# A planned attention-and-experts kernel: VectorE's two-operand steps, triangles by select, the 1e-9 and the sinks' products

## The chip, the cores and the metric

The kernel runs on one core of a Trainium2 chip. The metric is device time in microseconds of one execution. Before the change it is 349.83 us, the median of three runs (349.22 to 351.33).

A core has TensorE (PE, with PEld for its weight loads), VectorE (DVE), ScalarE (ACT), GpSimd (POOL) and SyncE (SP), which here only issues DMAs. Each engine works through its own instructions in program order and waits on semaphores for the others.

## What is computed

Two stages in float32. The first is attention with four sink keys and a window of 128 keys, for 4 batches and 8 heads of 64 over 768 positions. The second, over its output, is four causal attention experts of width 64, of which each row takes the two with the largest gate logits.

```python
keep = is_sink | in_window                      # 4 sinks, window 128
scores = np.where(keep, scale * q @ k.T, -1e9)
a = np.exp(scores - scores.max(-1))
a = a / (a.sum(-1) + 1e-09)
x = a @ v                                       # heads side by side: 768 x 512
...
topk = np.argpartition(-(x @ w_gate), 2)[..., :2]
w = np.exp(sel - sel.max(-1)); w /= w.sum(-1) + 1e-09
for e in range(4):                              # causal attention of each expert
    a = softmax_causal(scale * (x @ wq[e]) @ (x @ wk[e]).T)   # sum + 1e-09 too
    out += mask_e * w_e * (a @ (x @ wv[e]) @ wo[e])
```

## The kernel before

**Stages.** A unit of the first stage is a batch and a pair of heads (16 units): load q, k and v, turn them so that the head dimension lies on the partitions (on TensorE in batch 0, L679; by VectorE's 32x32 transposes later, L698), compute scores (L709 for rows 0 and 1, L726 for two rows at a time in the band), pick and mask on VectorE (L1113, L1119, L1057), exponentiate on ScalarE with the row sum (L1123, L1062), take the reciprocal (`factor`), normalise on GpSimd (L1143, L1077), turn the probabilities and multiply with v (L753). The result goes as a high and a residual part into x: L588 on ScalarE, L593 on VectorE. A unit of the second stage is a batch and a pair of experts: projections from x (L1232, three float32r products of high and residual parts each), scores (L717), mask (L975), exponential (L987), normalisation, products (L753), output projection (L1308) and store. Values and gate logits of all experts come from L1259.

**Weights.** Each weight is split as it arrives: ScalarE writes the high part (L531), then GpSimd or VectorE subtracts it from the staged weight to give the residual part (L538). In that subtraction both operands are in SBUF.

**The sum's reciprocal.** `factor` runs after every group of exponentials, 88 times. Its `go` on VectorE is a tensor_reduce (L772), which adds the row sum in column 1 of a small tile `st` to a constant 1e-9 in column 4, and then a reciprocal (L773). In the second stage a small GpSimd multiplication with the gate's weight follows (L776).

**The triangles.** Of a band's two key blocks, the nearer is needed once whole and once cut to its triangle. In 8 row pairs of batch 0 (`transposed_band`) TensorE turns the block and a select on GpSimd (L869, 128x256) or a multiplication on VectorE (L872) cuts it. The other 24 row pairs (`swapped_band`, batches 1 to 3) turn it by VectorE and a trip through DRAM; there one multiplication of 128x512 with a mask `swapped_own` cuts it (L921), 18 times on GpSimd and 6 times on VectorE.

**The sinks' products.** `of_sinks` (L758) adds the four sink keys' part: one or two matmuls of 128 lanes, of which lanes 64 and up hold zeros.

**The gate.** `weigh` (L1290 to L1294, VectorE) turns the kept logits' exponentials into weights; L1290 and L1294 have two SBUF operands. `rank` (L1281 and after, GpSimd) stands before it.

**What sets the order.** All work is cut into 2427 steps with a cost per engine that may run them. `ORDER` is a list of all steps' numbers; a letter behind a number puts the step on ScalarE (a), VectorE (v) or GpSimd (p) instead of the engine that its cost names first. `Plan.emit` goes through the list in order and writes each step's instructions into its engine's program; beside that it keeps a clock of its own from the costs, which decides only which buffer of a ring a step takes and where dummy matmuls fill TensorE's gaps in the first 130 us.

Of the kernel before, what the change touches and what calls it, by code (L numbers as in the profile page):

```python
# [10 lines left out]
F32 = mybir.dt.float32  # L11
# [3 lines left out]
OP = mybir.AluOpType  # L15
AX = mybir.AxisListType
# [146 lines left out]
class Step:  # L163


    def __init__(self, prio, cost, fn, after, new, use, moves, mode, behind, lag, besides, spared):
# [4 lines left out]
        for b in new:  # L171
            b.maker = self
# [15 lines left out]
class Plan:  # L188
# [1236 lines left out]
```

## Time and profile before

| | before |
|---|---|
| median of three runs | 349.83 us |
| the profiled execution | 349.71 us, span 348.0 us |
| TensorE busy | 337.1 us (97%) |
| VectorE busy | 294.4 us (85%) |
| ScalarE busy | 263.0 us (76%) |
| GpSimd busy | 210.8 us (61%) |
| TensorE's granted clock | 0.998 |
| DMA moved | 65.44 MB, 188 GB/s |

The span is the time from the first to the last instruction in the trace; 1.7 us of the execution lie around it. A row of the timeline gives start, duration, engine, line, operation, the tiles written and read, and in brackets how long the engine stood idle before it and who ended that. A row of a group gives total busy time, the mean of one in nanoseconds, and the idle time of the engine before its instructions. TensorE's matmuls are pipelined, so their durations overlap.

### The profile page before, as it was taken

The page shows a single profiled execution, that of the slowest core. Times are in us where ns is not written, and L with a number is a line of the kernel's source. Part 1 is how long each engine was busy: PE and PEld are TensorE (multiplying, and loading weights), DVE is VectorE, ACT ScalarE, POOL GpSimd, SP SyncE. Part 2 cuts the span into 40 slices and gives each one's busy share as a digit, 9 for nine tenths or more (in the row PEclk, how much of TensorE's full clock was granted, in tenths as well). Part 3 has the DMA queues.
Part 4 walks back from the last instruction along what each step waited for, and adds up shares of the span by engine and source line. Part 5 has one row for each costly group of instructions (what it writes and reads, how often), then busy time and mean ns, then how long its engine had stood idle before and what let it go on. Part 6 is the DMA issues. An engine that isn't in the chain of part 4 may idle for free.

```text
span 348.0 us, 12460 instructions
## 1 busy us (share of the span) xinstructions
PE 337.1 (97%) x4290; PEld 291.3 (84%) x4290; DVE 294.4 (85%) x1245; ACT 263.0 (76%) x874; POOL 210.8 (61%) x411
## 2 busy tenths in 40 slices
PE   8899899998989999999999999999999999999996
PEld 7677688986888799987888889977898899987885
DVE  5899999999899998899999888899987875579712
ACT  3899999968987986668969686499858964679922
POOL 7699798877767564677952734288984600144600
PEclk9999999999999999999999999999999999999999
DMA  7798799996977879769385989969785582037785
GB/s 232 176 218 130 104 153 170 202 208 182 235 221 187 238 190 198 210 147 166 114 267 136 190 244 167 218 174 229 250 252 158 197 259 65 2 122 216 224 277 194
DMA packets 159318, 65.44 MB, mean 188 GB/s; under 512 B 115856, under 2 KB 148880, under 8 KB 159256
## 3 DMA queue, kind: packets, MB, share of 16 engines
q1 hardware_dynamic: 158984, 64.53, 73.6%
q8 instruction: 34, 0.56, 0.7%
q14 instruction: 28, 0.23, 0.2%
q10 hardware_dynamic: 272, 0.13, 0.1%
HBM read 39.69 MB, written 24.90 MB: 186 GB/s over the span
## 4 chain that ended last, share of the span: by engine, by line
PE 78%; DVE 11%; ACT 3%; DMA 2%; issue 2%; POOL 1%; SPq 1%; DVEq 0%; ACTq 0%; POOLq 0%
PE b L1232 18%; PE b L753 17%; PE b L1259 10%; PE b L1308 9%; PE b L717 9%; PE b L784 5%; PE b L726 5%; PE b L709 2%; PE b L679 2%; DMA d<-n 2%; DVE p L1119 1%; PE b L758 1%; ACT n L1062 1%; DVE n L975 1%; DMA p<-d 1%
## 5 line engine op out<-in xcount | busy, mean ns | idle before, releaser
L1123 ACT ACTIVATE p<-p,st 128x132 f32<-128x132 f32 x128 | 50.9, 403 | 6.0 <-DVE st L1119 6.0
L1062 ACT ACTIVATE n<-n,st 128x128 f32<-128x128 f32 (+1 forms) x96 | 42.8, 449 | 4.9 <-DVE st L1057 4.9
L1077 POOL TENSOR_TENSOR n<-n,st 128x256 f32<-128x256 f32 (+2 forms) x50 | 35.0, 716 | 11.1 <-DVE st L773 9.1
L987 ACT ACTIVATE n<-n,st 128x768 f32<-128x768 f32 (+1 forms) x32 | 28.0, 876 | 16.4 <-DVE st L975 12.9
L717 PE MATMUL b<-ks,qs 64*128 64x384 f32 (+3 forms) x384 | 38.1, 333 | 0.9 <-DVE ks L653 0.9
L1259 PE MATMUL b<-wvh,x 128*128 128x260 f32 x192 | 36.6, 285 | 0.0
L753 PE MATMUL b<-n,v 128*64 128x128 f32 x544 | 34.7, 275 | 0.0
L1232 PE MATMUL b<-x,wqh 128*128 128x512 f32 (+1 forms) x128 | 33.5, 345 | 1.0 <-DVE st L975 1.0
L1308 PE MATMUL b<-woh,y 128*128 128x512 f32 (+1 forms) x100 | 34.2, 396 | 0.0
L1232 PE MATMUL b<-x,wkh 128*128 128x512 f32 (+1 forms) x128 | 33.7, 345 | 0.0
L1143 POOL TENSOR_TENSOR p<-p,st 128x512 f32<-128x512 f32 x32 | 33.2, 1040 | 0.0
L717 PEld LDWEIGHTS b<-ks,qs 64*128 64x128 f32 x384 | 30.2, 186 | 3.5 <-DVE ks L653 1.0
L605 ACT ACTIVATE n<-b 128x384 f32<-128x384 f32 (+2 forms) x65 | 27.5, 446 | 6.5 <-PE b L784 4.1
L1119 DVE CUSTOM_DVE_ANT_0 p<-b,pair_mask 128x132 f32<-128x132 f32 x128 | 32.1, 283 | 0.3
L753 PEld LDWEIGHTS b<-n,v 128*64 128x64 f32 x544 | 30.0, 137 | 2.3 <-issue 0.7
L824 DVE STREAM_TRANSPOSE n<-n 128x768 f32<-128x768 f32 (+1 forms) x32 | 28.3, 898 | 3.0 <-ACT n L995 3.0
L1259 PEld LDWEIGHTS b<-wvh,x 128*128 128x128 f32 x192 | 30.3, 188 | 0.7 <-DVE st L1057 0.4
L921 POOL TENSOR_TENSOR p<-p,swapped_own 128x512 f32<-128x512 f32 x18 | 23.3, 1295 | 11.4 <-DMA p<-d 10.4
L726 PE MATMUL b<-n,n 64*64 64x200 f32 (+1 forms) x512 | 27.0, 336 | 2.9 <-DVE x L593 1.5
L605 ACT ACTIVATE p<-b 128x256 f32<-128x256 f32 (+1 forms) x56 | 23.9, 449 | 7.7 <-PE b L1308 5.3
L698 DVE STREAM_TRANSPOSE n<-n 128x384 f32<-128x384 f32 x48 | 26.3, 560 | 2.4 <-DMA n<-in_k_dram 1.2
L1259 PE MATMUL b<-wvl,x 128*128 128x260 f32 x96 | 27.1, 282 | 0.0
(147 smaller groups left out, 1006.8 us busy)
## 6 DMA issues: line engine op xcount, KB each, us to landing
d<-n SPq DMA_DIRECT2D x24, 288.0 KB, 2.9
n<-in_v_dram SPq DMA_DIRECT2D x16, 384.0 KB, 4.6
p<-d SPq DMA_DIRECT2D x96, 64.0 KB, 2.5
d<-n SPq DMA_DIRECT2D x16, 384.0 KB, 2.6
n<-d SPq DMA_DIRECT2D x64, 96.0 KB, 2.8
out_dram<-p SPq DMA_DIRECT2D x23, 256.0 KB, 2.9
d<-n SPq DMA_DIRECT2D x16, 320.0 KB, 2.9
n<-d SPq DMA_DIRECT2D x64, 80.0 KB, 2.8
```

What stands on the lines that cost most here:

```text
L605: nc.scalar.activation(dst(), src(), AF.Copy)
L717: nc.tensor.matmul(o, self.qs.t[hs, a, qs], x, start=n == 0, stop=n == 2)
L726: nc.tensor.matmul(o[c:c + 64, 256 * r:256 * r + n], self.q_of()[hs, q:q + 64], self.ks.t[hs, 0, k:k + n], start=True, stop=True)
L753: nc.tensor.matmul(o[e * 64:e * 64 + 64], lhs, rhs, start=e not in self.begun, stop=last and self.done == len(self.steps))
L1062: nc.scalar.activation(x, x, AF.Exp, bias=st.t[:, 0, n:n + 1], scale=-1.0, accum_out=st.t[:, 1, n:n + 1])
L1077: nc.gpsimd.tensor_mul(x, x, f[:, :, None].to_broadcast([128, n, 128 * i + 128]))
L1119: nc.vector.tensor_tensor_reduce(out=p.t[:, n, :], in0=s2[e].t[:, 324 * r:324 * r + SW], in1=pair_mask, scale=-scale, scalar=BIG, op0=OP.a ...
L1123: nc.scalar.activation(p.t[:, n, :], p.t[:, n, :], AF.Exp, bias=st.t[:, 0, n:n + 1], scale=-1.0, accum_out=st.t[:, 1, n:n + 1])
L1143: nc.gpsimd.tensor_mul(p.t[:, :, :128], p.t[:, :, :128], f()[:, :, None].to_broadcast([128, 4, 128]))
L1232: nc.tensor.matmul(t.t, w[a][:, c, es], X[b, c].t[:, x, cs], start=c == 0 and m == 0, stop=c == NCH - 1 and m == 2)
L1259: nc.tensor.matmul(t.t[:, :VW], X[b, c].t[:, a, qs], W["wv"][w][:, c, :], start=c == 0 and n == 0, stop=c == NCH - 1 and n == 2)
L1308: nc.tensor.matmul(t.t[:, a0:z0], Y[b, c].t[:, a, qs], W["wo"][w][:, c, a0:z0], start=c == 0 and n == 0, stop=c == EP - 1 and n == 2)
```

## The change

Five things.

1. The planner's clock now treats a VectorE step with two SBUF operands (`port=True`: residual weights, the sinks' residual values, the gate's weights) as one that starts only when GpSimd's clock is free, and that keeps GpSimd for its length. The costs of these steps are smaller: 330 for 620, 1200 for 1900, 1000 for 1045.
2. The swapped rows' triangles are cut by two selects of 128x256 on GpSimd (L932 after the change); the mask `swapped_own`, its four copies and the option of VectorE go.
3. `factor` is two steps: a tensor_scalar that adds 1e-9 (L776 after the change), on VectorE or GpSimd, and the reciprocal on VectorE (L779). The list puts 39 of the 88 on VectorE and 49 on GpSimd.
4. A step of the sinks' products may carry the letter q: then it takes 64 lanes and counts as the tile shape of the score matmuls. 16 of the 32 carry it.
5. `ORDER` is a new list, of 2514 steps (88 more, and the mask's step less).

```diff
-46 4 48 54 55v 47 49 51 58 61 56v 132 52v 57 62v 53a 60a 66 59v 63a 67 134 71 133 218 69 140 137 304 73 139v 82 135 138v 83
+47 3 45 46 53 50 55a 48 51v 136 134 57 135 60 52a 54v 62a 58a 56 59v 61v 65 66 139 68 70 67 72 82 223 1 141a 83 88 69 142 108
...
-                s = self.steps[int(word.rstrip("avp"))]
+                s = self.steps[int(word.rstrip("avpq"))]
+                if word[-1] == "q":
+                    s.mode, s.cost = s.alt[0], {PE: s.alt[1]}
...
+            if e == DVE and s.port:
+                t = max(t, free[POOL])
+                free[POOL] = t + s.cost[e]
...
-    def mask_of_swapped():
-        for g in range(2):
-            for e in range(2):
-                to = swapped_own.rearrange("p (g h) (r e) c -> p g e h r c", g=2, r=2)[:, g, e]
-                nc.gpsimd.tensor_copy(to, own.rearrange("p (r h c) -> p h r c", r=2, h=2))
...
-                me.append(plan.step(prio + 3, {POOL: 160 + 2.05 * w + 190 * extra, DVE: 620 + 90 * extra}, low, after=[h], use=[st]))
+                me.append(plan.step(prio + 3, {POOL: 160 + 2.05 * w + 190 * extra, DVE: 330 + 90 * extra}, low, after=[h], use=[st], port=True))
...
-            nc.tensor.matmul(self.b.t[:, at:at + n], lhs, rhs, start=not self.begun, stop=last and self.done == len(self.steps))
+            nc.tensor.matmul(self.b.t[:, at:at + n], lhs[lanes], rhs[lanes], start=not self.begun, stop=last and self.done == len(self.steps))
...
+        def guard():
+            on = nc.gpsimd if guarded.eng == POOL else nc.vector
+            on.tensor_scalar(st.t[:, 2, :w], st.t[:, 1, :w], 1e-9, None, op0=OP.add)
+
         def go():
-            r = st.t[:, 2, :w]
-            nc.vector.tensor_reduce(r, st.t[:, 1:5:3, :w].rearrange("p r e -> p e r"), axis=AX.X, op=OP.add)
-            nc.vector.reciprocal(r, r)
-        s = plan.step(prio, {DVE: 285}, go, after, (), [st])
+            nc.vector.reciprocal(st.t[:, 2, :w], st.t[:, 2, :w])
+        guarded = plan.step(prio, {DVE: 140, POOL: 150}, guard, after, (), [st])
+        s = plan.step(prio, {DVE: 145}, go, [guarded], (), [st])
...
+            lanes = slice(0, 64 if wide.mode == "rows" else 128)
...
         def tri():
-            flat = lambda x: x.rearrange("p q n c -> p (q n c)")
-            (nc.gpsimd if cut_off.eng == POOL else nc.vector).tensor_mul(flat(pts[1].t), flat(pts[0].t), flat(swapped_own))
-        cut_off = plan.step(prio, {DVE: 70 + 1.04 * 512, POOL: 1250}, tri, [came] + OWN, [pts[1]], [pts[0]])
+            for g in range(2):
+                half = slice(2 * g, 2 * g + 2)
+                nc.gpsimd.affine_select(out=pts[1].t[:, half], in_=pts[0].t[:, half], pattern=[[32, 2], [64, 2], [0, 2], [1, 32]],
+                                        compare_op=OP.is_ge, fill=0.0, base=0, channel_multiplier=-1)
+        cut_off = plan.step(prio, {POOL: 800}, tri, [came], [pts[1]], [pts[0]])
...
-            WT_READY[b] += [[plan.step(prio, {DVE: 1045}, weigh, [s], (), [gate])]] * m
+            WT_READY[b] += [[plan.step(prio, {DVE: 1000}, weigh, [s], (), [gate], port=True)]] * m
...
-    SELECT_NS = 410
+    SELECT_NS = 375
```

Lines after L760 have moved by up to 12: L593 is L597, L698 is L702, L872 is L879, L1077 is L1089, L1113 is L1125 and L1119 is L1131 after the change.

VectorE before, where the residual of wk is made while batch 0's first stage runs (`x` is that stage's output, `st` the small tile of sums, `n` and `p` rows of scores or probabilities, `b` PSUM banks):

```order
L772 TENSOR_REDUCE st_126<-st_126 128x4
L773 RECIPROCAL st_126<-st_126 128x4
L698 STREAM_TRANSPOSE n_76<-n_76 128x384
L538 TENSOR_TENSOR wkl<-v_0_108,wkh 128x256
L593 SCALAR_TENSOR_TENSOR x_103<-b_128,x_103 128x512
L1119 ISA p_98,st_122<-b_131,pair_mask 128x132
L1119 ISA st_122 128x1
L698 STREAM_TRANSPOSE n_76<-n_76 128x384
L538 TENSOR_TENSOR wkl<-v_0_108,wkh 128x256
```

The same place after:

```order
L779 RECIPROCAL st_126<-st_126 128x4
L879 TENSOR_TENSOR p_85<-b_134,own 128x2x2x64
L879 TENSOR_TENSOR p_85<-b_129,own 128x2x2x64
L702 STREAM_TRANSPOSE n_79<-n_73 128x3x128
L1125 COPY_PREDICATED b_132<-nearer,b_132 128x2x64
L542 TENSOR_TENSOR wkl<-v_0_108,wkh 128x256 x2
L1125 COPY_PREDICATED b_135<-nearer,b_135 128x2x64
L597 SCALAR_TENSOR_TENSOR x_103<-b_128,x_103 128x256
L776 TENSOR_SCALAR st_127<-st_127 128x4
L779 RECIPROCAL st_127<-st_127 128x4
```

Three single subtractions, two of them next to a residual of x, became two in a row (the other two of wk are GpSimd's now), and the reduce before a reciprocal became a tensor_scalar, here or on GpSimd.

GpSimd before, where the first swapped triangles of batch 1 are cut and the gate of batch 0 is ranked:

```order
L1077 TENSOR_TENSOR n_69<-n_69,st_127 128x256
L1077 TENSOR_TENSOR n_75<-n_75,st_126 128x512
L1077 TENSOR_TENSOR n_69<-n_69,st_127 128x512
L921 TENSOR_TENSOR p_90<-p_95,swapped_own 128x512
L1023 TENSOR_TENSOR p_98<-n_68 128x512
L921 TENSOR_TENSOR p_82<-p_80,swapped_own 128x512
L1281 TENSOR_TENSOR gate_119<-gate_119 128x24
```

And after:

```order
L1089 TENSOR_TENSOR n_76<-n_76,st_123 128x256
L776 TENSOR_SCALAR st_126<-st_126 128x2
L1027 TENSOR_TENSOR vs_117<-vp,sel 64x128
L1089 TENSOR_TENSOR n_76<-n_76,st_123 128x512
L776 TENSOR_SCALAR st_124<-st_124 128x4
L776 TENSOR_SCALAR st_122<-st_122 128x2
L932 AFFINE_SELECT p_85<-p_80 128x256 x2
L1035 TENSOR_TENSOR p_90<-n_74 128x512
L1293 TENSOR_TENSOR gate_119<-gate_119 128x24
```

Each multiplication with the mask became two selects, and three small tensor_scalar stand between GpSimd's multiplications.

## Rows read from the trace of the kernel before

**Rows 1.** The page's first part: busy time, share of the span, instructions.

```profile
PE 337.1 (97%) x4290; PEld 291.3 (84%) x4290; DVE 294.4 (85%) x1245; ACT 263.0 (76%) x874; POOL 210.8 (61%) x411
```

**Rows 2.** Stretches: length, busy PE, PEld, DVE, ACT, POOL, clock, DMA share, GB/s.

```profile
0.00:12.00 12.00, 9.53 (x247) 8.21 (x251) 7.24 (x43) 5.72 (x20) 8.14 (x41) 1.00 0.84 231
...
24.00:36.00 12.00, 11.67 (x239) 9.18 (x237) 11.37 (x66) 12.00 (x54) 11.69 (x28) 1.00 0.96 146
36.00:48.00 12.00, 10.46 (x163) 8.11 (x158) 11.87 (x48) 10.36 (x46) 9.87 (x22) 1.00 0.80 128
...
180.00:192.00 12.00, 12.00 (x182) 10.92 (x179) 11.56 (x49) 9.49 (x28) 3.97 (x4) 1.00 0.64 172
...
336.00:348.00 12.00, 8.73 (x61) 6.87 (x59) 2.44 (x6) 2.45 (x5) 0.00 (x0) 0.95 0.60 221
```

**Rows 3.** TensorE's waits: for whom, us in total, times, longest.

```profile
PE b L726 <- issue: 1.3, 1, 1.3
PE b L1325 <- DVE nought L394: 1.1, 1, 1.1
```

**Rows 4.** Timeline of VectorE, 36 to 43 us.

```profile
36.74 2.93 DVE L538 TENSOR_TENSOR wkl<-v,wkh 128x256 fp32r<-128x256 f32 x1
39.59 0.68 DVE L593 SCALAR_TENSOR_TENSOR x<-b,x 128x512 fp32r<-128x512 f32 x1
...
40.90 0.38 DVE L538 TENSOR_TENSOR wkl<-v,wkh 128x256 fp32r<-128x256 f32 x1
```

**Rows 5.** Timeline of GpSimd, 18 to 40 us.

```profile
18.03 1.41 POOL L869 TENSOR_SCALAR_AFFINE_SELECT p<-p 128x256 f32<-128x256 f32 x1
...
36.34 1.11 POOL L869 TENSOR_SCALAR_AFFINE_SELECT p<-p 128x256 f32<-128x256 f32 x3
37.43 1.60 POOL L1077 TENSOR_TENSOR n<-n,st 128x256 f32<-128x256 f32 x2
38.99 0.40 POOL L869 TENSOR_SCALAR_AFFINE_SELECT p<-p 128x256 f32<-128x256 f32 x1
```

**Rows 6.** Timeline of TensorE: the three places where VectorE ends its wait.

```profile
40.33 0.54 PE L726 MATMUL b<-n,n 64*64 64x196 f32 x5 [1.54 <-DVE x L593]
...
80.85 0.74 PE L1232 MATMUL b<-x,wqh 128*128 128x512 f32 x2 [0.99 <-DVE st L975]
...
113.40 0.44 PE L753 MATMUL b<-p,p 128*64 128x128 f32 x4 [0.46 <-DVE p L921]
```

**Rows 7.** Timeline of VectorE and GpSimd around the gate's weights.

```profile
78.16 1.03 DVE L1290 SCALAR_TENSOR_TENSOR gate<-gate 128x24 f32<-128x24 f32 x1
...
78.11 1.04 POOL L1143 TENSOR_TENSOR p<-p,st 128x512 f32<-128x512 f32 x1
...
304.51 0.18 DVE L1290 SCALAR_TENSOR_TENSOR gate<-gate 128x24 f32<-128x24 f32 x1 [0.16 <-POOL gate L1286]
```

**Rows 8.** Groups by line and shape: busy us, mean ns, idle time before.

```profile
L758 PEld LDWEIGHTS b<-sk,vs 128*128 128x128 f32 x56 | 8.6, 189 | 3.1 <-issue 2.2 <-DVE st L975 0.2
...
L772 DVE TENSOR_REDUCE st<-st 128x4 f32<-128x8 f32 x56 | 8.4, 150 | 1.3 <-ACT p L1123 0.7 <-POOL p L1143 0.2
...
L869 POOL TENSOR_SCALAR_AFFINE_SELECT p<-p 128x256 f32<-128x256 f32 x14 | 6.4, 479 | 0.0
...
L921 DVE TENSOR_TENSOR p<-p,swapped_own 128x512 f32<-128x512 f32 x6 | 6.1, 1023 | 0.0
...
L776 POOL TENSOR_TENSOR st<-st,gate 128x2 f32<-128x2 f32 x32 | 6.0, 195 | 25.8 <-DVE st L773 20.4 <-DVE gate L1294 3.2 <-ACT x L588 1.1
...
L772 DVE TENSOR_REDUCE st<-st 128x2 f32<-128x4 f32 x32 | 4.6, 144 | 2.0 <-ACT n L987 1.1 <-ACT p L987 0.9
...
L1292 DVE TENSOR_SCALAR gate<-gate 128x6 f32<-128x6 f32 x4 | 0.7, 173 | 0.1
```

**Rows 9.** L921: count, then minimum, median and maximum in ns.

```profile
L921 POOL TENSOR_TENSOR p<-p,swapped_own x18: 1270/1294/1316, 70.2 to 270.4; 128x512 f32<-128x512 f32 x18
...
L921 DVE TENSOR_TENSOR p<-p,swapped_own x6: 684/1004/1435, 112.0 to 264.4; 128x512 f32<-128x512 f32 x6
```

More of the change, by code (lines that the diff above doesn't have):

```diff
@@ L163, with __init__ @@
 class Step:
-    def __init__(self, prio, cost, fn, after, new, use, moves, mode, behind, lag, besides, spared):
+    def __init__(self, prio, cost, fn, after, new, use, moves, mode, behind, lag, besides, spared, port, alt):
         self.prio, self.cost, self.fn, self.new, self.moves, self.mode = prio, cost, fn, new, moves, mode
@@ L170, in __init__ @@
         self.besides, self.spared = besides or {}, spared or {}
+        self.port, self.alt = port, alt
         for b in new:
@@ L195, in __init__, with step @@
         self.fifo = {}
-    def step(self, prio, cost, fn, after=(), new=(), use=(), fifo=None, moves=0, mode="FULL", behind=(), lag=0, besides=None, spared=None):
-        s = Step(prio, cost, fn, after, new, use, moves, mode, behind, lag, besides, spared)
+    def step(self, prio, cost, fn, after=(), new=(), use=(), fifo=None, moves=0, mode="FULL", behind=(), lag=0, besides=None, spared=None,
+             port=False, alt=None):
+        s = Step(prio, cost, fn, after, new, use, moves, mode, behind, lag, besides, spared, port, alt)
         for name in fifo if isinstance(fifo, tuple) else (fifo,) if fifo else ():
@@ L437 @@
                                 base=0, channel_multiplier=-1)
-        swapped_own = consts.tile([128, 4, 4, 32], F32, name="swapped_own")
     else:
@@ L578, in sink_values @@
         h = plan.step(SINK_VALUES + 1, {ACT: 60 + 0.833 * n}, lambda: nc.scalar.activation(vp, vr(), AF.Copy), [ld], (), [st])
-        lo = plan.step(SINK_VALUES + 1, {POOL: 2430, DVE: 1900}, low, [h], (), [st])
+        lo = plan.step(SINK_VALUES + 1, {POOL: 2430, DVE: 1200}, low, [h], (), [st], port=True)
         lows = [plan.step(SINK_VALUES + 2, {SP: 960}, bring, [lo], (), (), moves=400)]
@@ L754, in add, with add_wide @@
             self.begun.add(e)
[L756 removed]
+        def add_wide(self, i, n, lhs, rhs, last, lanes):
             at = (i - self.lo) * 128
[L758 removed]
+            nc.tensor.matmul(self.b.t[:, at:at + n], lhs[lanes], rhs[lanes], start=not self.begun, stop=last and self.done == len(self.steps))
             self.begun |= {0, 1}
@@ L883, in of_sinks @@
             acc.done += 1
+            lanes = slice(0, 64 if wide.mode == "rows" else 128)
             for n, x in enumerate(of_sk):
-                acc.add_wide(i + n, 256 // len(of_sk), vs.t.rearrange("p e d -> p (e d)"), x(), n + 1 == len(of_sk))
+                acc.add_wide(i + n, 256 // len(of_sk), vs.t.rearrange("p e d -> p (e d)"), x(), n + 1 == len(of_sk), lanes)
         new, used = acc.bufs()
-        acc.steps.append(plan.step(prio + AV_LAG - 0.01, {PE: 115 if len(of_sk) == 1 else 169}, of_sinks, [*moved_sk, made_vs], new, [sk, vs] + used,
-                                   fifo="av", mode="FULL"))
+        cost = 115 if len(of_sk) == 1 else 169
+        wide = plan.step(prio + AV_LAG - 0.01, {PE: cost}, of_sinks, [*moved_sk, made_vs], new, [sk, vs] + used, fifo="av", mode="FULL",
+                         alt=("rows", cost))
+        acc.steps.append(wide)
         def av():
```

189 lines of the change are left out of this document (97 added, 92 removed), and 3 rows, old and new, of the table ORDER.

## The prediction

> **What bounds the kernel now.** I read the page's busy shares first, then the stretches, then TensorE's own waits, then the timeline around the longest of them. TensorE is busy 337.1 of 348.0 us [rows 1], so whatever the change does for other engines counts only where TensorE stands idle. The reader should see in [rows 2] where that is: 2.5 us are missing from 12.0 in the first stretch, 1.5 in 36 to 48, 3.3 in the last, and nothing in 180 to 192. In 24 to 48 VectorE is busy 23.2 us of 24 and GpSimd 21.6, while at 180 to 192 GpSimd works 4.0 of 12 and TensorE alone sets the pace. The granted clock is 1.00 (the 2.4 GHz level) nearly throughout, so no time is to be had there. Of the 10.9 us of idle time, 1.1 lie before the first matmul [rows 3] and 3.3 in the last stretch [rows 2]; neither depends on what changes. 6.5 us can be won at most, as far as idle time goes.
>
> **Whom TensorE waits for.** Of its longer waits after the start, one of 1.3 us is put down to "issue", which is nothing that the profile shows [rows 3]. Three are VectorE's: 1.54 us of L726 for x, 0.99 of L1232 and 0.46 of L753 for L921 [rows 6]. All three lie right behind one kind of VectorE instruction.
>
> At 36.74 VectorE starts a subtraction for wk, both of whose operands are in SBUF, and takes 2.93 us [rows 4]. The next one, of the same shape, takes 0.38 at 40.90. From 36.34 on GpSimd works without a gap [rows 5]: three selects, two multiplications, a fourth select, which ends at 39.39; VectorE's subtraction ends 0.28 later. So the two engines exclude each other for this kind of instruction, and VectorE lost 2.55 us. Behind it on VectorE stood the residual of x (39.59), for which TensorE stood idle until 40.33.
>
> The gate's L1290 shows it again: 1.03 us at 78.16 beside GpSimd's 1.04 us L1143, and 0.18 us at 304.51 with GpSimd idle [rows 7]. That is 0.85 us, and TensorE's 0.99 follows at 80.85. L921 on VectorE takes 684 ns at best and 1435 at worst [rows 9].
>
> **The change, part by part.** The base is the profiled execution: 349.71 us, a span of 348.0 and 1.7 around it. It lies 0.1 below the median of 349.83.
>
> *The wk subtraction.* Two of four now stand on VectorE, back to back, where the planner took GpSimd to be free (330 ns instead of 620). The list fixes an order on each engine, not a time, so the wait can come back; as long as GpSimd's queue has no gap it can be 2.55 us again. I take it as gone: **−1.5 us** of TensorE, with bounds 0 and −1.5. The Trainium skill (SBUF — State Buffer, Who interferes with whom) has a VectorE instruction with two SBUF inputs contend with a GpSimd one that reads SBUF, and the second to issue block until the first is done. The trace agrees that they exclude each other, not on how long: by the rule a wait that comes back ends with the select under way (0.4 us, a sum of 346.4), by the rows it outlasts whatever GpSimd has ready (347.5).
>
> *The gate's weights.* Same instructions, planned behind GpSimd's. If L1290 costs 0.18 as at 304.51, 0.85 of 0.99 us go: **−0.85**, bounds 0 and −1.0.
>
> *The triangles of the swapped rows.* Six multiplications leave VectorE (6.1 us, mean 1023 ns) and 18 leave GpSimd (23.3 us); 48 selects of 128x256 come to GpSimd [rows 8, 9]. The nearest row is L869: 0.40 us at 38.99 [rows 5], 479 ns on average, raised by one of 1.41 us at 18.03. So 19.2 to 23.0 us. The form with four steps in its pattern is not in the trace; at twice L869's price it would add 19 us more, which I keep for the range. On VectorE the 0.46 us that TensorE lost to L921 at 113.40 go [rows 6]: **−0.46**, bounds 0 and −0.5. The mask's four copies (1.0 us of GpSimd) go too. They are counted at nothing, since TensorE's first projections lie beside them; −1.0 at most.
>
> *The 1e-9.* 88 tensor_reduce (8.4 + 4.6 us) become 39 tensor_scalar on VectorE and 49 on GpSimd. The only tensor_scalar of the kernel on VectorE, L1292, takes 173 ns [rows 8], so VectorE saves 13.0 − 6.7 = 6.3 us. GpSimd's small L776 takes 195 ns, so GpSimd gains 9.6 us of work, and the steps it holds get one more hop, ScalarE to GpSimd to VectorE to GpSimd, in which the small instruction stands behind multiplications of 1.04 us, as the rows of the two orders show. GpSimd in all: −23.3 + 19.2 (to 23.0) + 9.6 − 2.4 (five L869 fewer) − 1.0 = +2.1 to +5.9 us on 210.8. It has 39% of the span free, but next to none from 24 to 36 [rows 2]. Up to TensorE's first projection, 13 such steps stand in the list, 5 of them on GpSimd, so VectorE saves 5 × 0.15 = 0.8 us there, where it is busy 97%. I pass half on: **−0.4**, bounds −1.0 (VectorE's saving whole, and later hops hidden) and +1.5 (five GpSimd steps there, each behind one multiplication of 1.04 us, 0.3 of it not hidden).
>
> *Sinks' products on 64 lanes.* 16 of 32 steps carry the letter. The weight loads in front of L758 show 3.1 us of idle time [rows 8], 2.2 of it "issue"; half the steps bound the gain by 1.5 us. But counted along the two orders, TensorE changes its tile shape 153 times before and 155 after, so what those steps save others pay. **0**, bounds −1.5 and +0.5.
>
> *The order.* TensorE's matmuls are the same, three dummy fills against two. Of the 6.5 us of idle time, 2.9 are taken above. Of the other 3.6, an order that knows of GpSimd for VectorE's two-operand steps (15 before, 7 after) can take some: **−0.5**, bounds −2.5 and +2.5 (a new wait of the size of the largest old one). DMA issues are the same 226 rows in another order. The share of DMA is at 0.96 in 24 to 36, so a transfer that is moved behind others there may come late; that is part of the +2.5.
>
> Sum: 349.71 − 1.5 − 0.85 − 0.46 − 0.4 − 0.5 = **346.0 us**. From 180 on TensorE has no idle time to absorb it, so what is won before stays won.
>
> **The rivals.**
>
> *The waits are given back* (about 349). For it: the front is full on VectorE, GpSimd and DMA at once [rows 2], and GpSimd gets more small work just there; a stall that goes may uncover the next engine. Against it: the wk stall blocked VectorE alone, and ScalarE and GpSimd had their results ready. Half the sum's gain gone and 1.0 of guards in the way: 349.71 − 1.85 + 1.0 = 348.9.
>
> *The new tensor_scalar is itself held up by GpSimd* (slower). 18 of the 39 on VectorE stand in the first half of its rows, and up to 48 us GpSimd is busy 68 to 97% of the stretches shown [rows 2]. If each had to wait as the two-operand steps do, from L921's mean over its best (1023 − 684 = 0.34 us) [rows 8, 9] to L1290's 0.85, is the price: 6.1 to 15.3 us of VectorE. At the wk step 1.54 of 2.55 us reached TensorE, a share of 0.6: +3.7 to +9.2, so 349.7 to 355.2 on top of 346.0. From a mean wait of 0.65 us on (18 × 0.65 × 0.6 = 7.0) it is slower than before by 1%. Against it: none of the 88 reduces, of small SBUF operands too, shows such a wait (150 and 144 ns on average) [rows 8]. For it: no row decides, since the four L1292 ran while GpSimd was idle.
>
> The Trainium skill (SBUF — State Buffer, Who interferes with whom) says just this of a tensor_scalar: with one SBUF source and an SBUF destination it can enter a two-port mode and then contends with GpSimd, while a tensor_reduce never does. By that rule the replacement trades an instruction that can't be blocked for one that can; no run here shows it, and the planner doesn't mark this step as one that waits.
>
> *More than planned goes* (about 343). With VectorE lighter by 6.1 + 6.3 us, the other waits shrink too: another 2.5 to 3 of the 3.6. For it: VectorE ends most of TensorE's waits. Against it: the largest of those left is the 1.3 us of "issue" [rows 3].
>
> **How the numbers follow.** Forecast 0.52, its own range 344 to 348; given back 0.20; tensor_scalar held up 0.15; more 0.13. A little over half of the forecast (0.31) lies below 346.3, which is 1% under the median, about what a measurement of this kernel can tell from no change; with the 0.13 that makes faster 0.44. Slower by over 1% is half of the held-up case and a little of the others: 0.10. The rest is 0.46. The range leaves out one in ten on either side: 342.8 to 351.5.
>
> **What would show it.** Right: no VectorE instruction with two SBUF operands over about 0.8 us in the first 100 us; TensorE's wait in 36 to 48 under 0.5 us; L921's place in the profile is GpSimd's alone, with selects near 0.40 us; VectorE's total down by 10 to 14 us; the tensor_scalar near 0.15 us. Wrong: tensor_scalar on VectorE with a mean over 0.4 us beside a GpSimd instruction; GpSimd's guards late and VectorE's reciprocals waiting for them; selects at 0.8 us; new idle time of TensorE before 60 us that DMA ends.

## The result and the profile after

The changed kernel takes 346.39 us, the median of four runs (345.65 to 346.4), beside 350.58 for the kernel before on the same chip: a ratio of 0.9878 [0.9836, 0.9919]. Two more comparisons of the same program, on two chips, gave 0.9856 [0.9818, 0.9894] and 0.9887 [0.9849, 0.9925]. So it is faster by 1.1 to 1.4%; 346.0 was predicted.

The profiled execution took 345.65 us, with a span of 343.9. The page's first part (busy time, share of the span, instructions):

```profile
PE 336.1 (98%) x4292; PEld 292.9 (85%) x4292; DVE 285.6 (83%) x1198; ACT 263.1 (76%) x871; POOL 216.9 (63%) x481
```

Beside [rows 1], TensorE's idle time fell from 10.9 to 7.8 us, which is 3.1 of the 4.1 us of span; its busy time fell by 1.0. VectorE is lighter by 8.8 us, GpSimd heavier by 6.1.

Three stretches, columns as in [rows 2], and TensorE's waits, columns as in [rows 3]:

```profile
12.00:24.00 12.00, 10.60 (x270) 8.25 (x265) 11.88 (x63) 11.96 (x58) 9.43 (x20) 1.00 1.01 221
...
36.00:48.00 12.00, 12.00 (x209) 10.10 (x209) 11.69 (x52) 11.53 (x48) 11.01 (x22) 1.00 0.65 112
...
96.00:108.00 12.00, 11.22 (x178) 10.27 (x174) 11.41 (x47) 9.40 (x29) 5.46 (x14) 1.00 0.64 172
```

```profile
PE b L1337 <- DVE nought L405: 1.1, 1, 1.1
PE b L791 <- DVE st L1069: 0.9, 1, 0.9
PE b L757 <- DMA n<-in_v_dram: 0.8, 1, 0.8
PE b L791 <- POOL n L1089: 0.6, 1, 0.6
PE b L1244 <- DVE st L987: 0.3, 1, 0.3
```

The stretch from 36 to 48, where 1.5 us were missing, is full. None of the three waits of [rows 6] is there at its old size: the one for x is gone, the one for L921 too, and the gate's 0.99 is 0.3. In their place stand 0.9 us for VectorE's L1069, 0.8 for a transfer of v and 0.6 for GpSimd.

VectorE at the two places that the prediction speaks of, the residual of wk and the gate's weights (start, duration, engine, line, operation; x2 stands for two in a row):

```profile
40.24 0.77 DVE L542 TENSOR_TENSOR wkl<-v,wkh 128x256 fp32r<-128x256 f32 x2
...
41.13 0.41 DVE L597 SCALAR_TENSOR_TENSOR x<-b,x 128x256 fp32r<-128x256 f32 x1
...
76.98 0.63 DVE L1302 SCALAR_TENSOR_TENSOR gate<-gate 128x24 f32<-128x24 f32 x1
```

Two subtractions together take 0.77 us, where one of [rows 4] took 2.93. The gate's L1302 still takes 0.63 beside a GpSimd multiplication of 1.04 us.

What the prediction did not count on stands at 19.90 us. The first two rows are GpSimd's, the third VectorE's, the last two VectorE's next instruction and TensorE's wait:

```profile
19.75 0.41 POOL L876 TENSOR_SCALAR_AFFINE_SELECT p<-p 128x256 f32<-128x256 f32 x1
...
20.14 1.26 POOL L1035 TENSOR_TENSOR p<-n 128x512 f32<-128x512 f32 x1
...
19.90 1.52 DVE L776 TENSOR_SCALAR st<-st 128x4 f32<-128x4 f32 x1
...
21.34 0.28 DVE L1069 CUSTOM_DVE_ANT_0 n<-b,bmask 128x128 f32<-128x128 f32 x1
...
22.09 0.33 PE L791 MATMUL b<-ident,psk 64*128 64x64 f32 x3 [0.95 <-DVE st L1069]
```

The new tensor_scalar works on four numbers per partition and takes 1.52 us. It ends with GpSimd's multiplication, at 21.42 and 21.40, and has sat through a select before that. L1069 comes 1.4 us late, and TensorE waits 0.95 us for it. All instructions of that line (min, median and max in ns, first and last start), and its groups by shape with the selects (busy us, mean ns, idle time before):

```profile
L776 POOL TENSOR_SCALAR st<-st x49: 216/223/234, 10.3 to 318.9; 128x4 f32<-128x4 f32 x30, 128x2 f32<-128x2 f32 x19
L776 DVE TENSOR_SCALAR st<-st x39: 125/167/1523, 19.9 to 315.9; 128x4 f32<-128x4 f32 x26, 128x2 f32<-128x2 f32 x13
```

```profile
L932 POOL TENSOR_SCALAR_AFFINE_SELECT p<-p 128x256 f32<-128x256 f32 x48 | 21.0, 461 | 14.0 <-DMA p<-d 13.6
...
L776 DVE TENSOR_SCALAR st<-st 128x4 f32<-128x4 f32 x26 | 9.6, 374 | 2.8 <-ACT p L1135 1.8 <-ACT n L1074 0.9
...
L779 DVE RECIPROCAL st<-st 128x4 f32<-128x4 f32 x56 | 9.3, 167 | 3.1 <-POOL st L776 2.6
...
L762 PEld LDWEIGHTS b<-sk,vs 128*128 128x128 f32 x29 | 4.6, 188 | 1.8 <-issue 1.0 <-DVE p L879 0.3
L762 PEld LDWEIGHTS b<-sk,vs 64*128 64x128 f32 x27 | 4.3, 187 | 0.4 <-DVE st L779 0.2
...
L776 DVE TENSOR_SCALAR st<-st 128x2 f32<-128x2 f32 x13 | 3.1, 238 | 1.7 <-ACT n L999 1.7
```

On VectorE the 39 take 12.7 us. The 20 of them that start while a GpSimd instruction is running take 489 ns on average, the other 19 take 160 ns. All 13 that last longer than 0.2 us end 21 to 27 ns after an instruction of GpSimd. At their median of 167 ns they would take 6.5, so 6.2 us of VectorE go into waiting. The 88 reduces took 13.0 [rows 8], the 39 tensor_scalar take 12.7: VectorE gained nothing from this part.

### The profile page after: what moved, and what is told of

The parts are those of the page before. It is cut to its first block, busy times and chain, and to the rows that moved or that the text cites. A ratio compares the mean times of both kernels' runs of the same rounds, so it can differ in the third digit from the quotient of the medians.

```text
span 343.9 us, 12484 instructions
## 1 busy us (share of the span) xinstructions
PE 336.1 (98%) x4292; PEld 292.9 (85%) x4292; DVE 285.6 (83%) x1198; ACT 263.1 (76%) x871; POOL 216.9 (63%) x481
## 4 chain that ended last, share of the span: by engine, by line
PE 82%; POOL 6%; DMA 4%; DVE 2%; ACT 2%; issue 1%; SPq 1%; ACTq 0%; POOLq 0%; DVEq 0%
PE b L757 20%; PE b L1244 20%; PE b L1320 10%; PE b L1271 8%; PE b L721 7%; PE b L791 6%; PE b L730 5%; PE b L713 2%; PE b L762 2%; DMA n<-in_v_dram 1%; DMA n<-in_q_dram 1%; POOL n L1089 1%; DMA p<-d 1%; POOL p L1155 1%; SPq L1198 1%
## 5 line engine op out<-in xcount | busy, mean ns | idle before, releaser
L721 PE MATMUL b<-ks,qs 64*128 64x384 f32 (+3 forms) x384 | 39.6, 336 | 0.0
L1089 POOL TENSOR_TENSOR n<-n,st 128x256 f32<-128x256 f32 (+2 forms) x48 | 33.8, 714 | 4.9 <-DVE st L779 3.8
L776 POOL TENSOR_SCALAR st<-st 128x4 f32<-128x4 f32 (+1 forms) x49 | 11.0, 224 | 37.3 <-ACT n L999 19.2
L721 PEld LDWEIGHTS b<-ks,qs 64*128 64x128 f32 x384 | 31.1, 186 | 2.5 <-issue 0.7
L1244 PE MATMUL b<-x,wqh 128*128 128x256 f32 (+1 forms) x128 | 32.9, 342 | 0.3 <-DVE st L987 0.3
L1131 DVE CUSTOM_DVE_ANT_0 p<-b,pair_mask 128x132 f32<-128x132 f32 x128 | 32.2, 284 | 0.2
L757 PEld LDWEIGHTS b<-n,v 128*64 128x64 f32 x544 | 30.2, 137 | 2.1 <-issue 1.4
L609 ACT ACTIVATE n<-b 128x384 f32<-128x384 f32 (+2 forms) x65 | 26.7, 439 | 7.0 <-PE b L683 4.6
L1271 PEld LDWEIGHTS b<-wvh,x 128*128 128x128 f32 x192 | 30.2, 188 | 0.7 <-DVE st L1069 0.4
L932 POOL TENSOR_SCALAR_AFFINE_SELECT p<-p 128x256 f32<-128x256 f32 x48 | 21.0, 461 | 14.0 <-DMA p<-d 13.6
L609 ACT ACTIVATE p<-b 128x256 f32<-128x256 f32 (+2 forms) x53 | 22.4, 447 | 8.0 <-PE b L1320 7.3
L730 PE MATMUL b<-n,n 64*64 64x196 f32 (+1 forms) x512 | 27.4, 337 | 0.0
L702 DVE STREAM_TRANSPOSE n<-n 128x384 f32<-128x384 f32 x48 | 26.7, 563 | 0.8 <-DMA n<-in_k_dram 0.8
```

The costliest lines, as they stand in the source:

```text
L609: nc.scalar.activation(dst(), src(), AF.Copy)
L721: nc.tensor.matmul(o, self.qs.t[hs, a, qs], x, start=n == 0, stop=n == 2)
L730: nc.tensor.matmul(o[c:c + 64, 256 * r:256 * r + n], self.q_of()[hs, q:q + 64], self.ks.t[hs, 0, k:k + n], start=True, stop=True)
L757: nc.tensor.matmul(o[e * 64:e * 64 + 64], lhs, rhs, start=e not in self.begun, stop=last and self.done == len(self.steps))
L1089: nc.gpsimd.tensor_mul(x, x, f[:, :, None].to_broadcast([128, n, 128 * i + 128]))
L1131: nc.vector.tensor_tensor_reduce(out=p.t[:, n, :], in0=s2[e].t[:, 324 * r:324 * r + SW], in1=pair_mask, scale=-scale, scalar=BIG, op0=OP.a ...
```

## Experiments

Each ratio is against the kernel before, run in turn on the same chip, with its 95% interval.

**The same program again.** No edit.

> The changed kernel once more, on the chip and beside the runs that the next three share: 346.0 to 346.5 us by either theory, VectorE's 39 tensor_scalar at a mean of 0.33 us again (12.7 us in all), and TensorE's 0.95 us of idle time at 22 us behind the one that takes 1.52 us.

347.11 us beside 351.44, 0.9856 [0.9818, 0.9894]. That is 0.6 us over the time expected. The profiled execution took 348.15 us: its 39 tensor_scalar took 12.5 us, the long one 1.48, but TensorE, which had waited 0.96 us for a load of k at 6.9 us, waited 0.28 us behind it and not 0.95.

> The changed kernel, beside the runs that the next three share: 0.985 to 0.988 of the time before.

347.09 us beside 350.78, 0.9887 [0.9849, 0.9925]. Here the wait behind the long tensor_scalar is 0.90 us. Both ratios lie where the first comparison lay. The changed kernel's runs spread over 1.7 and 2.7 us in these two comparisons, so one profile can't decide less than that, and the verdicts below go by ratios. Where two edited kernels are compared, their medians are subtracted; taken from the ratios the differences come out up to 0.9 us otherwise.

**The 39 sums on VectorE as reduces again,** the 49 on GpSimd left as they are:

```diff
-            on = nc.gpsimd if guarded.eng == POOL else nc.vector
-            on.tensor_scalar(st.t[:, 2, :w], st.t[:, 1, :w], 1e-9, None, op0=OP.add)
+            if guarded.eng == POOL:
+                nc.gpsimd.tensor_scalar(st.t[:, 2, :w], st.t[:, 1, :w], 1e-9, None, op0=OP.add)
+            else:
+                nc.vector.tensor_reduce(st.t[:, 2, :w], st.t[:, 1:5:3, :w].rearrange("p r e -> p e r"), axis=AX.X, op=OP.add)
```

> The changed kernel, with the 39 tensor_scalar on VectorE written as the old tensor_reduce over the sum and the constant column; the 49 on GpSimd stay. Theory A (the tensor_scalar on VectorE excludes GpSimd's instructions, and this reaches TensorE): the 39 take 0.15 us each with no long ones, VectorE's busy time falls by about 6 us, TensorE's 0.95 us at 22 us go, and the time falls by 0.8 to 1.5 us. Rival B (the long ones are hidden, TensorE waits there for something else): busy time falls the same, the time by less than 0.3 us. Rival C (the long ones come from VectorE's queue, not from the kind of instruction): the reduces are as long, nothing changes.

345.96 us, 0.9828 [0.9785, 0.987], 1.15 us below the changed kernel beside it; their intervals overlap, so the difference is not shown. The trace shows what VectorE saves: groups of VectorE, then TensorE's longest wait in that run.

```profile
L778 DVE TENSOR_REDUCE st<-st 128x4 f32<-128x8 f32 x26 | 3.9, 154 | 2.5 <-ACT p L1137 1.6 <-ACT n L1076 0.9
L778 DVE TENSOR_REDUCE st<-st 128x2 f32<-128x4 f32 x13 | 1.8, 142 | 1.7 <-ACT n L1001 1.7
```

```profile
108.13 0.88 PE L757 MATMUL b<-n,n 128*64 128x128 f32 x12 [2.10 <-DMA n<-in_v_dram]
```

The reduces take 5.7 us where the tensor_scalar took 12.7, and TensorE's 0.95 us at 22 is gone. TensorE is then 1.4 us ahead of the first profiled execution of the changed kernel (the same matmul of the value projection starts at 68.79 and 70.18), but at 108 it waits 2.10 us for v instead of 0.78, and goes on at 108.13 where the other went on at 107.98. In the two later executions of the changed kernel this wait is 1.20 and 1.67 us, so it varies without any edit.

**All 88 sums on VectorE, as reduces and as tensor_scalar.** The list, the selects and the lanes stay.

```diff
-            on = nc.gpsimd if guarded.eng == POOL else nc.vector
-            on.tensor_scalar(st.t[:, 2, :w], st.t[:, 1, :w], 1e-9, None, op0=OP.add)
+            nc.vector.tensor_reduce(st.t[:, 2, :w], st.t[:, 1:5:3, :w].rearrange("p r e -> p e r"), axis=AX.X, op=OP.add)
```

> The changed kernel, with all 88 adds of 1e-9 as tensor_reduce on VectorE, at the places in the list where they stand. Against the one with 39 this puts 49 x 0.15 = 7.4 us on VectorE and takes 11 us off GpSimd. Theory A1 (taking adds off VectorE was part of the gain): 0.5 to 1.5 us slower than with 39 reduces. Rival B1 (GpSimd's extra hop costs as much as VectorE wins): within 0.4 us of it.

348.19 us, 0.9912 [0.9884, 0.994].

```diff
-            on = nc.gpsimd if guarded.eng == POOL else nc.vector
-            on.tensor_scalar(st.t[:, 2, :w], st.t[:, 1, :w], 1e-9, None, op0=OP.add)
+            nc.vector.tensor_scalar(st.t[:, 2, :w], st.t[:, 1, :w], 1e-9, None, op0=OP.add)
```

> The changed kernel, with all 88 as tensor_scalar on VectorE: the same places as with 88 reduces, one kind of instruction for the other. Theory A: many more are held up, since the 49 stand where GpSimd is busy; a mean of 0.3 to 0.4 us, 13 to 20 us of VectorE more than with reduces, and the time 2 to 6 us over that of 88 reduces. Rival B: under 0.5 us over it. Rival C: the two are alike.

355.68 us, 1.0114 [1.0076, 1.0152]: slower than the kernel before. The groups of the kernel with reduces, then of the kernel with tensor_scalar:

```profile
L775 DVE TENSOR_REDUCE st<-st 128x4 f32<-128x8 f32 x56 | 8.5, 153 | 6.6 <-ACT p L1134 3.5 <-ACT n L1073 2.2 <-ACT n L609 0.6
...
L775 DVE TENSOR_REDUCE st<-st 128x2 f32<-128x4 f32 x32 | 4.5, 146 | 5.1 <-ACT n L998 3.2 <-ACT p L998 1.8
```

```profile
L775 DVE TENSOR_SCALAR st<-st 128x4 f32<-128x4 f32 x56 | 22.5, 404 | 6.0 <-ACT p L1134 3.8 <-ACT n L1073 1.6 <-ACT n L609 0.4
...
L775 DVE TENSOR_SCALAR st<-st 128x2 f32<-128x2 f32 x32 | 7.7, 245 | 5.2 <-ACT n L998 3.1 <-ACT p L998 2.0
```

The two kernels differ in the form of one instruction. It costs VectorE 30.2 us instead of 13.0, and the kernel 7.5 us (7.1 by the ratios). That the tensor_scalar is held up by GpSimd is shown: the 50 that start while GpSimd works take 490 ns on average, the other 38 take 156, and the reduces at the same places 153 and 147. So is that giving 49 of the sums to GpSimd pays in this list: from all reduces (348.19) to 39 reduces (345.96) it is 2.2 us (3.0 by the ratios), and the intervals do not overlap. The changed kernel, with 39 of the bad form, stands between.

**The list alone.** The new list with the old steps: 88 reduces on VectorE, the mask's multiplication (all 24 on GpSimd), 128 lanes.

```diff
-                if word[-1] == "q":
-                    s.mode, s.cost = s.alt[0], {PE: s.alt[1]}
...
+            nc.vector.tensor_reduce(st.t[:, 2, :w], st.t[:, 1:5:3, :w].rearrange("p r e -> p e r"), axis=AX.X, op=OP.add)
...
+            nc.gpsimd.tensor_mul(flat(pts[1].t), flat(pts[0].t), flat(swapped_own))
```

> The new list with the old operations: all 88 adds as tensor_reduce on VectorE, triangles as one multiplication on GpSimd with the mask, 128 lanes. Against the run with 88 reduces alone (348.2 us) GpSimd's triangles take 24 x 1.30 = 31.1 us in place of 22.2. Theory A (the list, with VectorE's two-operand steps behind GpSimd's, brings most of the gain): 348 to 349.5 us, 2 to 3.4 under before. Rival B (the list only serves the new steps and brings nothing by itself): 350.5 us or more.

350.64 us beside 352.57, 0.9934 [0.9905, 0.9964]. The list brings 0.66%, about 2.3 of 350 us. TensorE now waits 1.7 us in two places for the mask's multiplication, which in the changed kernel is two selects:

```profile
PE b L760 <- POOL p L933: 1.7, 2, 0.9
```

**All products of the sinks on 128 lanes.** The changed kernel without the letter q.

```diff
-                if word[-1] == "q":
-                    s.mode, s.cost = s.alt[0], {PE: s.alt[1]}
```

> The changed kernel with all 32 sinks' products on 128 lanes (16 of them were on 64). Theory A (the shape's changes are moved, not saved): within 0.5 us of the changed kernel. Rival B (each of the 16 saves a change of tile shape on either side, some 0.1 us each): 1.5 to 3 us slower than it.

349.6 us beside 352.57, 0.9894 [0.9853, 0.9935]; the changed kernel has 0.9856 to 0.9887 in its three comparisons. No difference is shown. The mean of those is 0.9874, so the 64 lanes would be worth about 0.7 us, and with the width of the intervals anything up to some 2.4 us: Theory A is the likelier, but the lower edge of Rival B, 1.5 us, is not ruled out. By the forms of the weight loads in the traces, TensorE changes its tile shape 124 times in the changed kernel, 140 times without the letter and 128 times in the kernel before.

**The selects alone,** in the old list:

```diff
-            (nc.gpsimd if cut_off.eng == POOL else nc.vector).tensor_mul(flat(pts[1].t), flat(pts[0].t), flat(swapped_own))
+            for g in range(2):
+                half = slice(2 * g, 2 * g + 2)
+                nc.gpsimd.affine_select(out=pts[1].t[:, half], in_=pts[0].t[:, half], pattern=[[32, 2], [64, 2], [0, 2], [1, 32]],
+                                        compare_op=OP.is_ge, fill=0.0, base=0, channel_multiplier=-1)
```

> The kernel before with its old list, and all 24 triangles of the swapped rows as two selects on GpSimd at the places where the multiplications stood (the mask's copies stay). Theory A: VectorE loses 6.1 us of work, TensorE's 0.46 us at 113 go, and GpSimd loses 23.3 and takes 48 x 0.46 = 22.2 us: 0.3 to 0.8 us faster. Rival B (off the path): within 0.3 us. Rival C (six more waits for DMA in GpSimd's queue, 2.6 us each as in the four of before, hold its other work up): 0.5 to 2 us slower.

350.69 us beside 352.57, 0.9941 [0.9912, 0.9971]. That is 2.1 us [1.0 to 3.1], more than the 0.46 that TensorE was seen to wait for L921. The wait for x is still there in its trace:

```profile
40.56 1.00 PE L726 MATMUL b<-n,n 64*64 64x196 f32 x16 [1.95 <-DVE x L593]
```

**The wk subtraction out of VectorE's way,** in the kernel before, first try. The condition on the loop's variable never held when the step was written out, so this is the program of before a second time:

```diff
+                    if name == "wk" and a == 2:
+                        nc.vector.memset(of(lo).bitcast(F32), 0.0)
```

> The kernel before, with the wk subtraction that took 2.93 us at 36.74 replaced by a memset of the same tile on VectorE: same place, no SBUF operand to read (a quarter of wk's residual part is left out, so the output is a little less exact). Theory A (VectorE's wait for GpSimd there cost TensorE its 1.54 us, and what is won there stays won): no instruction over 0.5 us there, no idle time of TensorE at 40, and 1.0 to 1.6 us faster than before. Rival B (another engine is late right behind it): the idle time moves, under 0.4 us faster.

352.66 us beside 352.57, 0.9994 [0.9963, 1.0024]. It says nothing of wk, and only how well two equal programs agree. The second try replaces VectorE's three subtractions for wk with a memset:

```diff
+                    if on is nc.vector and name == "wk":
+                        nc.vector.memset(of(lo).bitcast(F32), 0.0)
```

> The kernel before, with VectorE's three wk subtractions replaced by memsets of the same tiles, this time in the program and not only in the text (the residual of three quarters of wk is left out of the result). Theory A (VectorE's 2.55 us behind GpSimd cost TensorE its 1.54 us, and what is won at 40 us stays won): no VectorE instruction over 0.7 us there, no wait of TensorE for x, and 1.0 to 1.7 us faster (0.995 to 0.997). Rival B (another engine is late right behind it): under 0.4 us.

349.77 us beside 350.78, 0.9969 [0.9941, 0.9997]: 1.1 us. VectorE at that place:

```profile
37.24 0.27 DVE L539 MEMSET wkl<- 128x256 f32 x1
37.43 0.63 DVE L596 SCALAR_TENSOR_TENSOR x<-b,x 128x512 fp32r<-128x512 f32 x1
```

The residual of x starts 0.2 us after the memset, and the matmul that waited until 40.33 [rows 6] starts at 39.13, without a wait. But the lead does not last. Equal matmuls stand in both programs, so their starts can be compared: TensorE of the kernel before, then of this one.

```profile
97.60 1.48 PE L717 MATMUL b<-ks,qs 64*128 64x128 f32 x17 [0.89 <-DVE ks L653]
...
268.46 1.67 PE L717 MATMUL b<-ks,qs 64*128 64x256 f32 x18
270.06 0.88 PE L753 MATMUL b<-n,n 128*64 128x128 f32 x12
...
309.46 0.39 PE L1308 MATMUL b<-woh,y 128*128 128x512 f32 x1
```

```profile
96.22 1.47 PE L720 MATMUL b<-ks,qs 64*128 64x128 f32 x17 [0.87 <-DVE ks L656]
...
267.61 2.28 PE L720 MATMUL b<-ks,qs 64*128 64x256 f32 x18
269.83 0.88 PE L756 MATMUL b<-n,n 128*64 128x128 f32 x12
...
309.38 0.39 PE L1311 MATMUL b<-woh,y 128*128 128x512 f32 x1
```

The lead is 1.38 us at 97, 0.85 at 268, 0.23 at 270 and 0.08 at 309. Some 0.4 us of it goes at 112.43, where the wait for VectorE's multiplication with the mask is 0.88 us and not the 0.46 of [rows 6]. At 268 the same 18 score matmuls take 2.28 us instead of 1.67. TensorE counts as busy all that time; the pause shows only in its weight loads (before, then this kernel) and in VectorE beside them:

```profile
268.46 1.35 PEld L717 LDWEIGHTS b<-ks,qs 64*128 64x128 f32 x18 [0.17 <-issue]
```

```profile
267.61 1.34 PEld L720 LDWEIGHTS b<-ks,qs 64*128 64x128 f32 x13 [0.17 <-issue]
269.10 0.47 PEld L720 LDWEIGHTS b<-ks,qs 64*128 64x128 f32 x5 [0.15 <-DVE y L596]
```

```profile
265.97 0.69 DVE L924 TENSOR_TENSOR p<-p,swapped_own 128x512 f32<-128x512 f32 x1 [2.37 <-DMA p<-d]
...
268.63 0.42 DVE L596 SCALAR_TENSOR_TENSOR y<-b,y 128x256 fp32r<-128x256 f32 x1
```

18 loads took 1.35 us before, here 13 take 1.34, and the 14th follows at 269.10, when VectorE's read of bank b for y (268.63 to 269.05) is over. That read was late because of a transfer: VectorE had stood 2.37 us waiting for the block that its last multiplication with the mask cuts, and worked without a gap from there to the read. In the first profiled execution of the kernel before, the block was there in time (the read starts at 268.57 there, with TensorE 0.85 us later):

```profile
264.40 0.69 DVE L921 TENSOR_TENSOR p<-p,swapped_own 128x512 f32<-128x512 f32 x1
```

The second execution of that program (the first try above, 353.9 us) settles whether TensorE's lead was the reason. TensorE came to this place 3.0 us later than in the first, and VectorE waited for the transfer and TensorE paused all the same; below them is the matmul that starts at 309.46 in the first:

```profile
269.73 0.69 DVE L924 TENSOR_TENSOR p<-p,swapped_own 128x512 f32<-128x512 f32 x1 [2.26 <-DMA p<-d]
...
271.48 2.18 PE L720 MATMUL b<-ks,qs 64*128 64x256 f32 x18
...
313.66 0.39 PE L1311 MATMUL b<-woh,y 128*128 128x512 f32 x1
```

So the pause goes with a transfer that is late against the rest, and it comes with or without the memsets. Beside this execution the kernel with memsets is 4.0 us ahead at 97 and 4.3 at 309, with nothing given back. One pair of traces doesn't tell how much of a lead stays.

**Both hold-ups and the triangles,** in the old list: the selects as above, and VectorE's subtractions for wk and wo as memsets.

```diff
+                    if on is nc.vector:
+                        nc.vector.memset(of(lo).bitcast(F32), 0.0)
```

> The kernel before with its old list, all 24 triangles as selects on GpSimd, and VectorE's three wk subtractions and its one of wo as memsets (those residual parts are left out of the result): no VectorE instruction with two SBUF operands is left but the sinks' residual and the gate's weights. If the selects' 2.1 us and wk's 1.5 us add up: 3.0 to 4.0 us faster than before (0.989 to 0.9915), the old list then nearly as good as the new one. If they are partly the same wait: 2.0 to 2.6 us.

349.06 us, 0.9954 [0.9924, 0.9984]. That is 1.6 us [0.6 to 2.7], where the two experiments before had 1.1 and 2.1. The interval leaves out the 3.0 us expected of gains that add. But each of the single gains is uncertain by a microsecond too, so that they do not add is likely and not shown. TensorE is 2.26 us ahead of the kernel before where that one waits for L921 (111.14 and 113.40), and then meets these:

```profile
132.81 0.50 PE L1237 MATMUL b<-x,wqh 128*128 128x256 f32 x2 [0.48 <-DVE n L610]
...
212.81 1.73 PE L756 MATMUL b<-n,v 128*64 128x128 f32 x24 [0.82 <-DMA n<-d]
...
309.40 0.39 PE L1313 MATMUL b<-woh,y 128*128 128x512 f32 x1
```

With the selects alone the same matmul of the output projection starts at 309.31. Four executions of programs with the old list reach it within 0.15 us. That says little of the programs: these four took 349.70 to 349.77 us, while their ratios go from 0.9941 to 1, and the second execution of the program of before reaches it at 313.66.

**v's load earlier,** on top of the kernel with 39 reduces: the load that TensorE waits for at 108 us goes ahead of another in the list.

```diff
-... 825 644 684 753 843p ... 883 1019 784 937 ...
+... 825 644 684 784 753 843p ... 883 1019 937 ...
```

> The changed kernel with the 39 adds on VectorE as tensor_reduce, and the load of the values that TensorE waits for at 106 us one step of the list earlier in SyncE's queue, ahead of five transfers. TensorE's wait for that load (0.8 us in the changed kernel, 2.1 with the reduces) should go: 1.5 to 2.5 us faster than the changed kernel (0.979 to 0.982 of before). Rival (the buffer that the earlier load takes is not free, and the queue behind it waits): no faster than with the reduces alone, 0.983.

346.18 us beside 350.78, 0.9885 [0.9837, 0.9933], where the changed kernel beside it has 0.9887: no faster. The wait for v is gone, and 1.07 us earlier stands one for the triangles' transfer:

```profile
107.06 0.44 PE L745 MATMUL b<-p,n 128*64 128x128 f32 x4 [0.67 <-DMA p<-d]
```

TensorE also waits 0.9 us for a load of k at 6.2 us. No version that was run is shown to beat the changed kernel. The one with 39 reduces came out ahead (0.9828), but this one, which has the same 39 reduces, did not.

## Why the prediction was right, and where it was not

The time was right to 0.4 us, and its sign came from the cause named: waits of TensorE that VectorE ended behind instructions held up by GpSimd. Taking the hold-ups at wk and wo and the multiplications with the mask off VectorE in the old list gives 1.6 us [0.6 to 2.7], where the sum has 1.96 for wk and the mask. That the whole came out so near is in part luck, since steps of the sum were wrong in opposite directions.

*What bounds the kernel.* TensorE's idle time could give 6.5 us, and about 3 were won there. One sentence does not hold as it stands: that from 180 us on TensorE has no idle time to absorb it, so that what is won before stays won. A stretch with a busy share of 100% can hold a pause: the row of 18 matmuls took 0.5 to 0.6 us longer in two of the three traces that have VectorE's last multiplication there, and counts as busy. How much of a lead is lost that way stays open. With the memsets for wk, a lead of 1.38 us at 97 beside one execution of the kernel before is down to 0.08 at 309; beside the other a lead of 4.0 us is still whole there.

*The wk subtraction, −1.5.* It came as planned: no stall, 0.77 us for two, 12.00 of 12 us busy from 36 to 48. Alone it was worth 1.1 us [0.1 to 2.1], an interval that holds the 1.5 too. The stall did not return, so this place doesn't say how long a returning one would last. The new one at 19.90 does: it outlasted the select under way by 1.26 us, as the rows had it. On this the Trainium skill (SBUF — State Buffer, Who interferes with whom) has the second to issue block until the first is done, and the measurement differs.

*The gate's weights, −0.85.* VectorE got 0.4 back, not 0.85: L1302 is 0.63 us beside a multiplication, not 0.18. TensorE's wait behind it fell by 0.7 all the same. No run changes this step alone.

*The triangles, −0.46.* The direction was right, the size too small: the selects alone gave 2.1 us [1.0 to 3.1] in the old list. The sum counted only the wait that the trace put down to L921, at 113.40. The 6.1 us that VectorE got rid of beside it were costed at nothing, and so was that a multiplication on VectorE can stand there waiting for its transfer: 2.26 and 2.37 us in two of the three traces that have it at 264 to 270, with TensorE's row of 18 matmuls at 2.18 and 2.28 us. With the selects alone that row takes 1.67, as in the execution that had no such wait. That is some 0.5 us more; where the rest comes from was not separated. The select of four steps takes 461 ns, within the 19.2 to 23.0 us given for all (21.0); 0.40 each was too low.

*The 1e-9, −0.4.* The sign was right and the size too small (all reduces 348.19, the changed kernel 347.11: 1.1 us, or 2.0 by the ratios, whose intervals overlap a little), and it comes this near only because two errors work against each other. The step that failed is "VectorE saves 13.0 − 6.7 = 6.3 us", priced by the four L1292 that ran beside an idle GpSimd. The 39 cost 12.7, and VectorE saved 0.3. In exchange the 49 sums on GpSimd, costed mainly as a hop that may delay, are worth 2.2 us or more. The rival *held up by GpSimd* describes what happened, at the lower edge of its price: 6.2 us of VectorE for a price of 6.1 to 15.3. It did not make the kernel slower because of its second factor. In the changed kernel 1.15 of 5.4 us of VectorE (285.2 and 279.8 busy in the two runs) reached the time, a share of 0.2 that is not clear of noise; with all 88 on VectorE it is 7.5 of 14.4 us, or 0.5. I took 0.6. What I held against the rival, that 88 reduces never wait, was true and beside the point: the reduces don't wait in the same places where the tensor_scalar does (153 and 404 ns, 56 of each).

The Trainium skill (SBUF — State Buffer, Who interferes with whom) says that a tensor_scalar with SBUF on both sides can contend with GpSimd and a tensor_reduce never does. The measurement agrees on both: 404 and 153 ns.

*Lanes, 0.* The traces have 128 changes of tile shape before and 124 after, where the prediction counted 153 and 155 along the orders. Nothing measured speaks against the 0: no difference is shown, and up to some 2.4 us could hide in the intervals.

*The order, −0.5.* The list alone gave 2.3 us [1.3 to 3.3], with the wk, gate and L921 waits gone in it; those three terms and −0.5 were 3.3. Selects and lanes on top of it, put at 0 once L921 had left VectorE, gave 0.8 (0.9934 to 0.9912), which the intervals don't separate from nothing. Together with 1.1 for the 1e-9 (2.0 by the ratios) that is 4.2 to 5.1, where the forecast had 3.7. The order's −0.5 cannot be told from the three terms in it.

Of the signs named ahead, VectorE's total was to fall by 10 to 14 us and fell by 8.8, which was the trace's hint at the tensor_scalar; the sign of a tensor_scalar with a mean over 0.4 us beside a GpSimd instruction came true (0.49); GpSimd's guards do make reciprocals wait (3.6 us in 6 places), and none of them ends one of TensorE's listed waits; DMA ends one of 0.8 us, at 108 and not before 60. The sign that no VectorE instruction with two SBUF operands takes over 0.8 us in the first 100 us was too tight: the sinks' residual values (`vp`) take 1.22 us at 12.54, and took as long in the kernel before.

## What to carry to other kernels

Price an instruction by a row in which the other engine is at work: a 0.17 us row beside an idle GpSimd said nothing of the 1.52 us beside a busy one, and the form that reads a constant column (tensor_reduce) was the cheaper one for VectorE. To see whether a lead lasts, compare starts of equal matmuls at several places, not only the wait that went, and do it against two executions of the unchanged program: here they were 4.2 us apart at the same matmul, and a pause that looked like the price of a lead stood in one of them too. And where several parts feed one pool of idle time, run them one by one and together: here 1.1 and 2.1 us gave 1.6, each give or take a microsecond.

## What was not expected of the hardware

- A tensor_scalar on VectorE with four fp32 numbers per partition waits for GpSimd: mean 404 ns over 56 beside 153 for a tensor_reduce at the same places, and up to 1620 ns in the three executions of the changed kernel.
- The exclusion seems to work both ways. While VectorE's pair for wk ran (40.24 to 41.01), a GpSimd multiplication of 128x16 took 0.46 us, in all three executions of the changed kernel; its median is 0.22:

```profile
40.28 0.46 POOL L1151 TENSOR_TENSOR psk<-psk 128x16 f32<-128x16 f32 x1
...
42.79 0.22 POOL L1151 TENSOR_TENSOR psk<-psk 128x16 f32<-128x16 f32 x1
```

- A select of 128x256 with four steps in its pattern takes 461 ns, the one of L876 405.
